# Four more units of y through DRAM, and the loads of turned k and q issued by ScalarE

## The chip, the cores and the metric

The kernel runs on one core of one Trainium2 chip. The metric is the device time of one execution in microseconds (us).

## The reference

Two blocks follow each other. The first is an mLSTM cell with gates, over 4 batches, 8 heads, 768 time steps and 40 values per head; the second is a feed-forward block on the 3072 tokens that come out, 320 values each.

```python
for t in range(S):
    m_new = np.maximum(f_gate[:, :, t] + m, i_gate[:, :, t])
    f_stab, i_stab = np.exp(f_gate[:, :, t] + m - m_new), np.exp(i_gate[:, :, t] - m_new)
    C = f_stab * C + i_stab * outer(v_t, k_t);  n = f_stab * n + i_stab * k_t
    h = C @ q_t;  denom = np.maximum(np.abs(n @ q_t), 1.0)
    y[:, :, t] = sigmoid(o_gate[:, :, t]) * h / denom
x = y as (3072, 320)
out = (((x @ w1) * (x @ w2)) @ w3) @ w_out        # w1, w2: 320 x 1024, w3: 1024 x 1024, w_out: 1024 x 320
```

All is float32.

## The kernel before

**Units and stages.** The tokens are cut into 24 units (n = 0 to 23) of 128 tokens: unit n is chunk n // 4 of batch n % 4. Four units make a group (gr = n // 4) of 512 tokens. One loop runs over stages s = 0 to 31. On TensorE, stage s does in this order: `x_trans` of an earlier unit (tile px, three 128x128 transposes), `fold` (tile wp: w3 times w_out, eight blocks of it in all), `up` and `up_rest` for groups 0 to 2 (tiles pa and pb), then `quarter_work(s)`: the output of unit s − 1 (tile cell, from pw, v and the state) and the scores and state products of unit s. So y of unit n leaves VectorE (line 445) in stage n + 1. TensorE's order is written down (`in_order`): each of its instructions follows the one before in the program. The other engines also run their instructions in the order in which they stand.

**The up products.** In stages 6 to 15 there are two `up` calls each. A call reads the turned x (tile xT) of two units at once: stages 12 and 13 read units 8 and 9, stages 14 and 15 units 10 and 11. Groups 3 to 5 are multiplied from stage 19 on by `up_by_seven` (a seven-product scheme), which needs sums of xT that `token_sums` makes on VectorE (line 666) when the group's last unit is turned. `up_by_seven` and `ffn_out` share the PSUM banks of the tile cell: ScalarE copies two products out of cell[1] (lines 704 and 702), after which `ffn_out` writes there.

**Two ways to turn y.** Units 0 to 14 go by `x_trans`: GpSimd repeats the last 64 columns (`twice`, line 476), TensorE transposes into PSUM (px, line 95), ScalarE copies to xT (line 486). In stages 10 and later `x_trans(n)` stands at the start of stage n + 3. Units 15 to 23 (`NY = 15`) go through DRAM: in stage n + 2, `send` writes y to y_d with four DMAs (lines 456 and 458), `get_back` reads it as 32-row blocks with four DMAs (tile yb, line 465), and `x_turn` transposes the blocks on VectorE (line 472). `x_turn` stands right before `turn(s + 1)`.

**Turned k and q.** From unit 10 on, `load_turned(n)` brings k and q in with eight DMAs (line 148), into one of two buffers (gates for even n, q_all for odd n), and `turn(n)` transposes them on VectorE (line 317). `load_turned(s + 2)` stands at the end of stage s, behind ScalarE's work of that stage: the a_sb copies (line 638), eight exponentials (pw, line 303), the gate (o_in, line 270) and, in stages up to 13, the scaling of raw weights (lines 191 and 195).

**Queues.** SP issues all loads and y_d transfers; ScalarE issues the stores of the output (line 743, `ffn_out`, from stage 16). In the built program the DMAs of both queues share eight completion counters, dealt out in turn. Each DMA carries a wait for the DMA that held its counter before.

Of the kernel before, what the change touches and what calls it, by code (L numbers as in the profile page):

```python
# [8 lines left out]
FP = mybir.dt.float32  # L9
# [7 lines left out]
def kernel(  # L17
# [26 lines left out]
    nc = tc.nc  # L44
# [3 lines left out]
    P = 128  # L48
    NT = S // L
    NT2 = S // P  # L50
    NU = NT2 * B
    NP = H // 2
# [16 lines left out]
    dram = ctx.enter_context(tc.tile_pool(name="dram", bufs=1, space=bass.MemoryType.DRAM))  # L69
# [7 lines left out]
    def mps(shape, name):  # L77
        pool = banks.pop(0)
        banks.append(pool)
        return pool.tile(shape, FP, name=name, tag="m")  # L80
# [13 lines left out]
    def transpose(out, in_, n=P):  # L94
        in_order(nc.tensor.transpose(out, in_, ident[0:n, 0:n]))  # L95
# [15 lines left out]
    N_DVE = N_U = 10  # L111
# [11 lines left out]
    decay = const.tile([P, B * NP, NT], FP, name="decay")  # L123
    UT = const.tile([P, 2, 3, BH], FP, name="UT")
    U_d = dram.tile([NT, BH, L], FP, name="U_d")
    NY = 15
    KC = KF + 1
    y_d = [dram.tile([P, 4, KC, 32], FP, name=f"y_d{n}") if n >= NY else None for n in range(NU)]

    o_t, u_t = {}, {}  # L130

# [9 lines left out]
    def load_turned(n):  # L141
        c, b = divmod(n, B)
        for dst, src in zip(turned_in[n % 2], (k, q)):
            for hip in range(2):
                of = src[b].rearrange("(p two) s d -> two p s d", two=2)[hip, :, c * P:(c + 1) * P, :]
                for j in range(2):
                    p0, c0 = hip * DP + j * 32, (1 - j) * 32
                    nc.sync.dma_start(out=dst[p0:p0 + 32, c0:c0 + NP * RAW].rearrange("r (p e) -> r p e", p=NP),  # L148
                                      in_=of.rearrange("p (r f) d -> r p (f d)", f=4))

    def load_o(n):
# [141 lines left out]
    def rows_of_u(n):  # L293
        c, b = divmod(n, B)
        nc.vector.transpose(out=weights_tile(n).rearrange("p h (t i) -> p h t i", t=2),
                            in_=UT[:, :, (0, 2, 1)[c], b * H:(b + 1) * H].rearrange("p t h -> p h t").unsqueeze(3).to_broadcast([P, H, 2, 32]))
# [14 lines left out]
    def turn(n):  # L311


        if n >= N_DVE:
            for src, dst, name in zip(turned_in[n % 2], (kT_t, qT_t), ("kT", "qT")):
                dst[n] = sb.tile([128, NP, P], FP, name=name, tag=name)
                done = nc.vector.transpose(out=dst[n].rearrange("i p (r f) -> i p f r", f=4),
                                           in_=src[:, 32:TB].rearrange("i (p f d) -> i p f d", p=NP, f=4)[:, :, :, 0:32])
            return done
        for src, dst, name in ((kbuf[n % NB], kT_t, "kT"), (qbuf[n % NBQ], qT_t, "qT")):  # L320
            pt = mps([128, NP, P], "pt")
            for p in range(NP):
                transpose(pt[:, p, :], src[:, 2 * p:2 * p + 2, :].rearrange("p a b -> p (a b)"))
            dst[n] = sb.tile([128, NP, P], FP, name=name, tag=name)
            nc.scalar.copy(out=dst[n], in_=pt)
# [7 lines left out]
    def decayed(new, old, n, x):  # L333
        c, b = divmod(n, B)
        nc.gpsimd.tensor_tensor(out=new, in0=old, op=OP.mult, in1=decay[:, b * NP:(b + 1) * NP, 2 * c + x:2 * c + x + 1]  # L335
                                .to_broadcast([P, NP, D1]))
# [114 lines left out]
    def send(n):  # L451


        y = y_t.pop(n)
        for cc in range(KF):
            nc.sync.dma_start(out=y_d[n][:, :, cc, :], in_=y[:, cc * P:(cc + 1) * P].rearrange("t (i c) -> t i c", c=32))
        for i in range(0, 4, 2):
            nc.sync.dma_start(out=y_d[n][:, i:i + 2, KF, :], in_=y[:, KF * P:DM].rearrange("t (i c) -> t i c", c=32))
# [3 lines left out]
    def get_back(n):  # L462
        back_t[n] = sb.tile([P, 4, KC, 32], FP, name="yb", tag="yb", bufs=1)
        for i in range(4):
            nc.sync.dma_start(out=back_t[n][32 * i:32 * (i + 1)].rearrange("r m k c -> r m (k c)"),
                              in_=y_d[n][:, i].rearrange("(m r) k c -> r m (k c)", r=32))

    def x_turn(n):
        gr, j = divmod(n, GT)
        if j == 0:  # L470
            x_t[gr] = ffn.tile([128, KC, TG], FP, name="xT", tag="xT")
        nc.vector.transpose(out=x_t[gr][:, :, j * P:(j + 1) * P].rearrange("c k (m r) -> c k m r", r=32),
                            in_=back_t.pop(n).rearrange("r m k c -> r k m c"))

    def twice(n):
        nc.gpsimd.tensor_copy(out=y_t[n][:, DM:DM + REM], in_=y_t[n][:, KF * P:DM])

    def x_trans(n):
        gr, j = divmod(n, GT)
        if j == 0:  # L480
            x_t[gr] = ffn.tile([128, KF + 1, TG], FP, name="xT", tag="xT")
        y = y_t.pop(n)
        px = mps([128, KF + 1, P], "px")
        for cc in range(KF + 1):
            transpose(px[:, cc, :], y[:, cc * P:(cc + 1) * P])
        nc.scalar.copy(out=x_t[gr][:, :, j * P:(j + 1) * P], in_=px)
# [5 lines left out]
    RAW = 4 * D  # L492
# [168 lines left out]
    def token_sums(gr):  # L661
        mem = wst.tile([128, FO, 128], FP, name="w3T", tag="w3T").rearrange("p k c -> p (k c)")
        T1, T2, T3, T4 = T_t[gr] = [mem[:, i * TH:(i + 1) * TH] for i in range(4)]
        (B11, B12), (B21, B22) = ([x_t[gr][:, cc, i * TH:(i + 1) * TH] for i in range(2)] for cc in range(KF))
        for dst, p, q in ((T1, B12, B11), (T2, B22, T1), (T3, B22, B12), (T4, B21, T2)):
            nc.vector.tensor_tensor(out=dst, in0=p, in1=q, op=OP.subtract)  # L666
# [96 lines left out]
    def ab_sums(gr, j):  # L763
        mem = [t.rearrange("p h d -> p (h d)") if j == 0 else io.tile([P, H, L], FP, name="pw", tag="pw", bufs=5)
               .rearrange("p h t -> p (h t)") for t in kbuf]
        S1, S2, S3, S4 = S_o[gr, j] = [t.rearrange("p (f t) -> p f t", t=P) for t in mem]
        (A11, A12), (A21, A22) = quarters_of_ab(gr, j)
        for dst, p, q, op in ((S1, A21, A22, OP.add), (S2, S1, A11, OP.subtract), (S3, A11, A21, OP.subtract),
                              (S4, A12, S2, OP.subtract)):
            nc.vector.tensor_tensor(out=dst, in0=p, in1=q, op=op)  # L770
# [47 lines left out]
    turned, converted, fetched = 0, 2, 5  # L818

    for s in range(len(n_up)):  # L820
        if NY <= s - 2 < NU:
            send(s - 2)
        if N_U <= s + 3 < NU:
            load_u(s + 3)
# [17 lines left out]
        if s < NU:  # L842
            if s >= B:
                decayed(state[s % B][1], state[s % B][0], s, 0)
        if s == 2 or N_DVE < s < NY + 2:
            twice(s - 2)
        if NY <= s - 2 < NU:
            get_back(s - 2)
        while s >= N_DVE and turned < min(s - 2, NY):
            x_trans(turned)  # L850
            turned += 1
        fold()
        if s >= len(n_up) - 2:
# [64 lines left out]
        with tc.issue_after(gated.ins) if gated else nullcontext():  # L918
            if seven:
                seven[3]()  # L920
            for _ in range({NU: 1, NU + 1: 3}.get(s, 0)):
                next(wsums)
            if s == NU + 1:
                ab_sums(*summed.pop(0))
            if NY <= s - 2 < NU:
                x_turn(s - 2)
            for n in () if s == 1 else (s + 2,) if s < B else (s + 2, s + 3) if s == B else (s + 3,):
                if n < N_U:
                    rows_of_u(n)
            if N_DVE <= s + 1 < NU:  # L930
                gated = turn(s + 1)
            if s - 2 in range(4 * GT - 1, NU, GT):
                token_sums((s - 2) // GT)
            if s < len(n_up) - 2 and n_out[s + 1] and s > NU + 2:
                ab_sums(*summed.pop(0))
# [8 lines left out]
        if s in (2, 3):  # L944
            turned, converted = 2, converted + (4 if s == 2 else 2)
        if s + 1 < N_DVE:
            while turned < min(s - 1, NY):
                x_trans(turned)
                turned += 1
            if s not in (1, 2):  # L950
                turn(s + 1)
# [22 lines left out]
        if N_DVE <= s + 2 < NU:  # L974
            load_turned(s + 2)
# [36 lines left out]
```

## Time and profile before

| | us |
|---|---|
| median of 3 runs | 425.77 |
| lowest and highest | 424.96, 426.05 |
| span of the profiled execution | 425.8 |
| TensorE busy | 414.1 |
| VectorE busy | 313.5 |
| GpSimd busy | 154.3 |
| ScalarE busy | 150.1 |
| mean share of the 16 DMA engines, SP's queue | 53.9% |

The profiled execution's span (first to last instruction) stands beside the median of the runs: they are the same to the digits shown. In the profile PE is TensorE's matmuls, PEld its weight loads, DVE VectorE, ACT ScalarE, POOL GpSimd, SP the engine that mostly issues DMAs; SPq and ACTq are DMA issues on these engines, and L with a number is a line of the kernel. Between 157 and 203 us a stage takes 15.3 us, in which TensorE is busy throughout.

### The profile page before, as it was taken

The page shows a single profiled execution, that of the slowest core. Times are in us where ns is not written, and L with a number is a line of the kernel's source. Part 1 is how long each engine was busy: PE and PEld are TensorE (multiplying, and loading weights), DVE is VectorE, ACT ScalarE, POOL GpSimd, SP SyncE. Part 2 cuts the span into 40 slices and gives each one's busy share as a digit, 9 for nine tenths or more (in the row PEclk, how much of TensorE's full clock was granted, in tenths as well). Part 3 has the DMA queues.
Part 4 walks back from the last instruction along what each step waited for, and adds up shares of the span by engine and source line. Part 5 has one row for each costly group of instructions (what it writes and reads, how often), then busy time and mean ns, then how long its engine had stood idle before and what let it go on. Part 6 is the DMA issues. An engine that isn't in the chain of part 4 may idle for free.

```text
span 425.8 us, 13079 instructions
## 1 busy us (share of the span) xinstructions
PE 414.1 (97%) x5353; PEld 335.3 (79%) x5353; DVE 313.5 (74%) x635; ACT 150.1 (35%) x404; POOL 154.3 (36%) x211
## 2 busy tenths in 40 slices
PE   7989989999999999999999999999999999999996
PEld 4768878888688788787777778788778879888896
DVE  6676986888949779778736966596868699575971
ACT  4766865567723623630433313032311110210000
POOL 4421342233303303303307751546453587542100
PEclk9989999999999999999999999999999999999999
DMA  8999998598977776985425675756421120000001
GB/s 186 204 173 245 214 144 140 134 193 180 215 183 154 166 182 135 181 164 105 89 80 130 153 141 121 142 133 117 87 44 36 35 39 2 31 2 31 2 32 62
DMA packets 135211, 51.15 MB, mean 120 GB/s; under 512 B 109360, under 2 KB 126960, under 8 KB 135152
## 3 DMA queue, kind: packets, MB, share of 16 engines
q1 hardware_dynamic: 131552, 46.29, 53.9%
q10 hardware_dynamic: 3600, 4.03, 2.7%
q8 instruction: 42, 0.69, 0.7%
q14 instruction: 17, 0.14, 0.1%
HBM read 44.50 MB, written 5.80 MB: 118 GB/s over the span
## 4 chain that ended last, share of the span: by engine, by line
PE 53%; issue 20%; DVE 7%; POOL 7%; SPq 7%; DMA 5%; ACT 1%; POOLq 0%; DVEq 0%
PE cell L92 17%; PE pa L92 12%; PE o L92 8%; PE pb L92 8%; PE p L92 3%; POOL pw L308 3%; SPq L184 3%; DVE w3T L666 2%; PE pt L95 1%; POOL vw L330 1%; SPq L148 1%; DMA raw<-in_moe_w_dram 1%; PE fill L92 1%; POOL raw L659 1%; POOL state L335 1%
## 5 line engine op out<-in xcount | busy, mean ns | idle before, releaser
L335 POOL TENSOR_TENSOR state<-state,decay 128x164 f32<-128x164 f32 x40 | 20.0, 500 | 154.8 <-DVE state L404 129.0
L92 PE MATMUL pa<-xT,w 128*128 128x256 f32 x240 | 60.4, 382 | 0.0
L92 PEld LDWEIGHTS pa<-xT,w 128*128 128x128 f32 x240 | 44.4, 190 | 6.8 <-DVE h L430 0.4
L303 ACT ACTIVATE pw<-pw,aT 128x64 f32<-128x64 f32 x184 | 46.4, 339 | 3.2 <-ACT o_sb L741 1.9
L92 PE MATMUL pb<-xT,w 128*128 128x256 f32 x192 | 45.4, 379 | 0.0
L729 POOL TENSOR_TENSOR ab<-ab,a_sb 128x512 f32<-128x512 f32 x22 | 29.4, 1356 | 32.2 <-DVE ab L684 32.2
L92 PEld LDWEIGHTS pb<-xT,w 128*128 128x128 f32 x192 | 36.4, 190 | 5.0
L711 POOL TENSOR_TENSOR wo<-wo 128x512 f32<-128x512 f32 x22 | 27.4, 1268 | 29.8 <-DVE wo L686 29.8
L92 PE MATMUL pa<-xT,wr 64*64 64x256 f32 x384 | 37.0, 386 | 0.5 <-DVE wr L200 0.5
L92 PE MATMUL wp<-wo,w3T 128*128 128x320 f32 x128 | 35.9, 433 | 1.1 <-DVE ab L639 0.6
L308 POOL TENSOR_SCALAR_AFFINE_SELECT pw<-pw 64x512 f32<-64x512 f32 x48 | 35.8, 746 | 3.0 <-ACT pw L303 1.2
L92 PE MATMUL pb<-xT,wr 64*64 64x256 f32 x384 | 36.4, 380 | 0.0
L92 PE MATMUL cell<-w3o,ab 128*128 128x320 f32 x128 | 35.4, 432 | 0.0
L638 ACT ACTIVATE a_sb<-pa 128x512 f32<-128x512 f32 x24 | 14.3, 598 | 59.0 <-PE pb L92 59.0
L639 DVE TENSOR_TENSOR ab<-pb,a_sb 128x512 f32<-128x512 f32 x24 | 16.4, 688 | 23.2 <-ACT a_sb L638 22.8
L92 PEld LDWEIGHTS wp<-wo,w3T 128*128 128x128 f32 x128 | 23.8, 190 | 10.5 <-DVE ab L639 0.8
L92 PEld LDWEIGHTS cell<-w3o,ab 128*128 128x128 f32 x128 | 24.3, 190 | 9.5
L92 PEld LDWEIGHTS pa<-xT,wr 64*64 64x64 f32 x384 | 18.9, 132 | 15.4 <-issue 8.8
L686 DVE SCALAR_TENSOR_TENSOR a_sb<-pa,wo 128x512 f32<-128x512 f32 x12 | 8.3, 689 | 29.8 <-PE pa L92 29.8
L430 DVE TENSOR_TENSOR h<-cell,h 64x164 f32<-64x164 f32 x88 | 28.6, 326 | 1.6
L92 PE MATMUL po<-w3o,ab 128*128 128x320 f32 x96 | 26.4, 433 | 0.0
L92 PEld LDWEIGHTS po<-w3o,ab 128*128 128x128 f32 x96 | 18.1, 190 | 7.3
(180 smaller groups left out, 846.4 us busy)
## 6 DMA issues: line engine op xcount, KB each, us to landing
raw<-in_moe_w_dram SPq DMA_DIRECT2D x64, 128.0 KB, 3.4
kbuf<-in_k_dram SPq DMA_DIRECT2D x24, 160.0 KB, 4.5
v_all<-in_v_dram SPq DMA_DIRECT2D x24, 160.0 KB, 4.9
o_in<-in_o_gate_dram SPq DMA_DIRECT2D x24, 160.0 KB, 4.8
pw<-U_d SPq DMA_DIRECT2D x28, 128.0 KB, 3.5
raw<-in_moe_w_dram SPq DMA_DIRECT2D x5, 512.0 KB, 6.7
raw<-in_moe_w_out_dram SPq DMA_DIRECT2D x8, 320.0 KB, 4.1
gates<-in_k_dram SPq DMA_DIRECT2D x28, 80.0 KB, 2.5
```

Source lines behind the costliest of these rows:

```text
L92: in_order(nc.tensor.matmul(out, lhsT=lhsT, rhs=rhs, start=start, stop=stop))
L184: nc.sync.dma_start(out=dst, in_=src)
L303: nc.scalar.activation(out=pw[:, h, :], in_=src[:, h, :], func=AF.Exp, bias=aT[:, c, b * H + h:b * H + h + 1])
L308: nc.gpsimd.affine_select(out=pw[r], in_=pw[r], compare_op=OP.is_ge, fill=0.0, base=0, pattern=[[0, H], [1, L]], channel_multiplier=-1)
L335: nc.gpsimd.tensor_tensor(out=new, in0=old, op=OP.mult, in1=decay[:, b * NP:(b + 1) * NP, 2 * c + x:2 * c + x + 1] .to_broadcast([P, NP, D1]))
L430: nc.vector.tensor_tensor(out=part, in0=ph[x][halves[e]], in1=part, op=OP.add)
L638: nc.scalar.mul(out=a_sb, in_=pa, mul=UP ** -2)
L639: nc.vector.tensor_tensor(out=ab_t[gr][j][:, fs[0]:fs[-1] + 1, t0:t0 + a_sb.shape[-1]], in0=pb, in1=a_sb, op=OP.mult)
L666: nc.vector.tensor_tensor(out=dst, in0=p, in1=q, op=OP.subtract)
L686: nc.vector.scalar_tensor_tensor(out=out, in0=p, scalar=UP ** -2, in1=q, op0=OP.mult, op1=OP.add)
L711: aside_by.tensor_tensor(out=kept[j][:, 1:4:2], in0=kept[j][:, 1:3], in1=kept[j][:, 3:4].to_broadcast([128, 2, TH]), op=OP.add)
L729: aside_by.tensor_tensor(out=t[:, f:FO:FH, :], in0=t[:, f:FO:FH, :], in1=a, op=OP.mult)
```

## The change

Unit 10 and units 12 to 14 join units 15 to 23 on the way through DRAM (`Y_BACK`), so of the units from 10 on only unit 11 still goes by `x_trans`. `x_turn` moves from before `turn(s + 1)` to behind it, for all units that go this way. The eight DMAs of `load_turned(n)` are issued by ScalarE instead of SP for n from 13 on.

```diff
-    NY = 15
+    Y_BACK = [10] + list(range(12, NU))
     KC = KF + 1
-    y_d = [dram.tile([P, 4, KC, 32], FP, name=f"y_d{n}") if n >= NY else None for n in range(NU)]
+    y_d = [dram.tile([P, 4, KC, 32], FP, name=f"y_d{n}") if n in Y_BACK else None for n in range(NU)]
...
-                    nc.sync.dma_start(out=dst[p0:p0 + 32, c0:c0 + NP * RAW].rearrange("r (p e) -> r p e", p=NP),
+                    (nc.sync if n < 13 else nc.scalar).dma_start(out=dst[p0:p0 + 32, c0:c0 + NP * RAW].rearrange("r (p e) -> r p e", p=NP),
                                       in_=of.rearrange("p (r f) d -> r p (f d)", f=4))
...
-        if NY <= s - 2 < NU:
+        if s - 2 in Y_BACK:
             send(s - 2)
...
-        if s == 2 or N_DVE < s < NY + 2:
+        if s == 2 or N_DVE < s < NU + 2 and s - 2 not in Y_BACK:
             twice(s - 2)
-        if NY <= s - 2 < NU:
+        if s - 2 in Y_BACK:
             get_back(s - 2)
-        while s >= N_DVE and turned < min(s - 2, NY):
-            x_trans(turned)
+        while s >= N_DVE and turned < min(s - 2, NU):
+            if turned not in Y_BACK:
+                x_trans(turned)
             turned += 1
...
-            if NY <= s - 2 < NU:
-                x_turn(s - 2)
             for n in () if s == 1 else (s + 2,) if s < B else (s + 2, s + 3) if s == B else (s + 3,):
                 if n < N_U:
                     rows_of_u(n)
             if N_DVE <= s + 1 < NU:
                 gated = turn(s + 1)
+            if s - 2 in Y_BACK:
+                x_turn(s - 2)
...
-            while turned < min(s - 1, NY):
+            while turned < s - 1:
                 x_trans(turned)
                 turned += 1
```

## The prediction

> **What bounds the kernel now.** I read the page first: who is busy, and where.
>
> ```profile
> span 425.8 us, 13079 instructions
> ...
> PE 414.1 (97%) x5353; PEld 335.3 (79%) x5353; DVE 313.5 (74%) x635; ACT 150.1 (35%) x404; POOL 154.3 (36%) x211
> ```
>
> TensorE is busy for 414.1 of 425.8 us, so a gain is work taken off it and a loss is a wait put before it. ScalarE's 35% is a mean; what matters is when its results are due. So next come the timelines of TensorE and ScalarE where stage 13 ends and stage 14 begins. Columns: start us, us, line, what, xcount, and in brackets the idle time before.
>
> ```profile
> 174.22 0.55 PE L95 MATMUL px<-ident,y 128*128 128x128 f32 x3
> 174.61 4.47 PE L92 MATMUL wp<-wo,w3T 128*128 128x320 f32 x16
> 178.92 1.89 PE L92 MATMUL pa<-xT,w 128*128 128x256 f32 x8
> ...
> ```
>
> ```profile
> 177.08 0.67 ACT L195 ACTIVATE raw<-raw 128x512 uint32<-128x512 uint32 x1
> 177.64 0.46 ACT L486 COPY xT<-px 128x384 f32<-128x384 f32 x1
> ```
>
> TensorE transposes y of unit 11 (px), does wp, and at 178.92 reads the xT that ScalarE has copied by 178.10. Margin: 0.82 us. Stage 12 has the same with unit 9: copy 146.35 to 146.82, pa at 148.34, margin 1.52 us. `up` reads the tokens of two units, so in the stages where a pair begins (12 and 14) nothing of it can start without this copy.
>
> Third, what a DMA costs the engine that issues it, in the view of waits of SP and ScalarE's timeline:
>
> ```profile
> SPq L465 <- DMA out_dram<-o_sb: 11.0, 4, 4.8
> ```
>
> ```profile
> 240.41 0.34 ACTq L743 DMA_DIRECT2D out_dram<-o_sb  x1
> 240.87 2.02 ACT L303 ACTIVATE pw<-pw,aT 128x64 f32<-128x64 f32 x8 [0.49 <-DMA y_d<-y]
> ```
>
> SP's reads of y_d waited 11.0 us for stores of the output, and ScalarE beside one of its own stores for a write of y_d; the data have nothing to do with each other. It is the eight completion counters: an issue stands until the earlier holder of its counter, on either queue, has landed. What stands behind it on that engine stands too.
>
> **The change part by part.**
>
> *TensorE loses 12 transposes.* The steps from px to the next matmul are 0.38 us for unit 10 (158.94 to 159.32) and 0.39 us each for units 12, 13 and 14 (189.51, 204.80, 220.07). TensorE has no idle time there, so all of it counts: −1.55 us, in stages 13, 15, 16 and 17.
>
> *ScalarE loses four xT copies* (0.47 us) and GpSimd four copies of 0.24 us. Neither set the end there: 0.
>
> *VectorE gains four transposes* of 0.57 us (5.1 us / 9 in the group L472). They lie in stages 12, 14, 15, 16, before VectorE's idle times of 2.15, 2.13, 7.59 and 3.53 us: 0. Without that cover they would cost 2.3 us together.
>
> *x_turn behind k and q* for units 15 to 23. One instruction changes places with two; before L666 their sum is the same, so TensorE's wait for L666 (0.41 us at 242.83) stays. The 1.40 us that VectorE waited for yb at 249.54 are hidden by 2 us of k and q, but VectorE then waits 4.87 us for TensorE anyway: 0.
>
> *SP* loses 88 issues (11 units x 8) of 0.45 us and gains 32. It has room: it waits 18.7 us for y alone. The four new sends do enter a queue that ran ahead: send(12) waits for y(12), and what stands behind it (loads for two stages later, get_back) follows late but in time.
>
> *ScalarE gains the 88 issues.* This is the part with a price. In the order of the built program the eight of unit 13 stand between the last `raw` and the xT copy of unit 9, those of unit 15 between `raw` and the copy of unit 11. One costs 0.45 us (four took 1.80 us on SP in quiet stages) and lands 2.4 us after issue, if its counter is free.
>
> Stage 12. The first five follow each other from 146.40; the last three use counters of the first three of the same eight and wait for those to land. The third is issued at 147.30, lands at 149.7 (2.4) or 150.8 (3.5, the k loads' median at 140 to 190 us); then the eighth issues, 0.45, and the copy, 0.47. Copy done at 150.6 to 151.7 against 148.34: 2.3 to 3.4 us. I take 2.6, nearer to the first, since half of the eight are q loads, which landed in 2.3.
>
> Stage 14, in times of before (y(12), ScalarE and TensorE all move with the shift). The last two of the eight use counters held before by the third and fourth DMA of send(12). These start only when y(12) leaves VectorE at 179.30 (L445, 178.48 + 0.82): two issues of 0.64, one of 0.57, the fourth at 181.15, issue over at 181.7. It lands 1.8 us after its start or its end: 183.0 to 183.5. Then 0.45 for the eighth issue, 0.46 for the copy, 0.1 for passing on: 184.0 to 184.5 against 178.92, so 5.1 to 5.6 us; I take 5.2. If no counter were waited for, 8 x 0.45 − 0.82 = 2.8 us.
>
> Stages 13, 15 and 16: only the wp copy stands behind the eight. Its bank is wanted 5 us later: 0.
>
> Stage 19: ScalarE's copy of the first product (L704) runs from 247.02 to 247.62, and TensorE writes that bank at 248.55, a margin of 0.93. Behind the eight of unit 20 (4.65 us, the last on a counter of the batch's fifth: 1.8 + 2.4 + 0.45) after o_in at 243.26, L704 ends at 248.5, just in time. But o_in will be later: pw stands behind an output store whose counter load_u(21) held, and that is issued behind send(16), whose y comes at 235.83. Sends to 238.6, landing 3.5, store 0.4, pw and o_in 2.4: 244.9; + 4.65 + 0.6 = 250.2 to 250.5, so 1.9 us of wait; between 0 (store not held) and 3.5 (a second store held as well). Stages 20 to 22 have this margin without two stores in a row: 0, at most 2 together.
>
> *The clock after a wait.* The windows show TensorE's busy time, granted clock, DMA share and GB/s:
>
> ```profile
> 21.00:24.00 3.00, 1.81 (x32) 0.90 1.14 129
> 24.00:27.00 3.00, 3.00 (x34) 0.53 1.03 160
> 27.00:30.00 3.00, 3.00 (x65) 1.00 0.99 153
> 57.00:60.00 3.00, 1.51 (x62) 1.00 0.60 82
> 60.00:63.00 3.00, 3.00 (x19) 1.00 1.23 220
> ```
>
> After 1.19 us of idle at 21.8 the clock was halved for some 3.4 us, which costs half of it, 1.7 us; after 1.49 us at 57.6 it was not. So short waits sometimes pay this. I put one such period behind the longest wait: 1.7 us; bounds 0 and 3.4.
>
> The Trainium skill, "TensorE: Matmul & The Clock Gate", section "What's actually happening", lets the clock fall only after a whole idle window of about 3.4 us; the row at 24.00 speaks against it. By that rule the waits of stages 12 and 19 cost nothing more, and that of stage 14 the same 1.7.
>
> Sum: 425.8 − 1.55 + 2.6 + 5.2 + 1.9 + 1.7 = 435.6 us. The span is the median (425.77), so no correction.
>
> A rule speaks against the move as such. The skill's "DMA: Bandwidth & Descriptors", section "Issuing engines are not separate DMA queues", says that issuing from more engines saves only the sequencer's time, usually small beside the transfer. Read as "issuing costs nothing worth counting", it would leave the sum at 424.2; by the rows above it does not hold here, because the issues stand in front of a copy that TensorE waits for.
>
> **The rivals.**
>
> *Faster, 424.2 us.* The copies still come in time, and only the −1.55 remains. Decided by the eight issues: they must take under 0.82 us in stage 14, 0.10 each, and under 1.52 us in stage 12. For it: ScalarE is only 35% busy, and it was always ahead of pa. Against it: ScalarE's own stores took 0.34 us each before any wait.
>
> *Issues, but no waits for counters: 428.3 us.* Eight issues take 2.7 us at the 0.34 of ScalarE's stores or 3.6 at SP's 0.45. Stage 12 loses 1.2 to 2.1 us, stage 14 1.9 to 2.8, less 1.55, clock and stage 19 at 0: 427.3 to 429.2. For it: most counters will be free. Against it: the SP row above, and send(12) cannot be early.
>
> *Waits everywhere: 442 us.* Stage 12 at 3.4, stage 14 at 5.7, stage 19 at 3.5, 2 in stages 20 to 22, two halved clocks of 1.7: 425.8 − 1.55 + 14.6 + 3.4 = 442.
>
> That the change does not do what it says is excluded by the built order, which shows the twelve transposes gone and the 88 issues on ScalarE.
>
> **How the numbers follow.** Forecast (waits for counters and for send(12), 432 to 438.5): 0.70. Waits everywhere (over 438.5): 0.12. No waits for counters (427.1 to 432): 0.11. Faster: 0.05. Within 0.3%: 0.02. 0.3% is 1.28 us, about what a measurement of this kernel can tell from no change (the three runs span 1.09 us). The predicted time is the forecast's, 435.6. The range leaves out the faster case and a little at each end: 429 to 441. Slower by over 0.3%: 0.70 + 0.12 + 0.11 = 0.93.
>
> **What would show it.** Right: TensorE idle before the first pa of stages 12 and 14, released by ScalarE's L486, 2 to 3 and 5 to 6 us; eight L148 issues on ScalarE ahead of that copy; the copies of stages 13 and 15 without effect; some idle before the cell<-w3o,ab of stage 19; four px groups gone. The forecast is wrong if TensorE's idle time stays near 11 us (the faster rival), if the stage 14 wait is under 3 us (the counter did not hold ScalarE), or if the loss lies on VectorE, waiting for yb.

## The result and the profile after

| | before | after |
|---|---|---|
| median, us | 425.91 (4 runs beside those of after) | 442.09 (4 runs, 440.60 to 445.37) |
| ratio of the times, 95% interval | | 1.040 (1.036 to 1.044) |
| profiled execution: span, us | 425.8 | 443.6 |

The change makes the kernel slower by 16 us. The forecast was 435.6 us and its range ended at 441: the direction was right, and so was the kind of loss (DMA issues on ScalarE in front of copies that TensorE waits for); the size was not. The profiled execution of after took 445.37 us, 1.8 us more than its span; the steps below compare span with span, 425.8 with 443.6.

The page of after, span and busy time of each engine:

```profile
span 443.6 us, 13121 instructions
...
PE 419.5 (95%) x5341; PEld 337.7 (76%) x5341; DVE 315.3 (71%) x639; ACT 149.0 (34%) x400; POOL 154.6 (35%) x207
```

TensorE runs 12 instructions fewer and is busy for 5.4 us longer (414.1 before). That can't be work, so part of it must run at a lower clock. Its idle time grew by 12.4 us (443.6 − 419.5 against 425.8 − 414.1). The view of waits says behind what; its columns are us in total, times, longest:

```profile
PE pa L92 <- ACT xT L486: 7.3, 2, 5.8
PE cell L92 <- ACT wo L702: 4.6, 1, 4.6
PE pa L92 <- DVE w3T L666: 0.4, 1, 0.4
```

The first two lines are new, the third was there before. To see in which stages the time is lost, take the start of `quarter_work(s)` on TensorE (the group cell<-v_all,pw) in both timelines, and its distance to the next one:

| from quarter_work of | before, us | after, us | difference |
|---|---|---|---|
| stage 11 (start) | at 141.13 | at 142.84 | +1.71 |
| 11 to 12 | 15.99 | 17.87 | +1.88 |
| 12 to 13 | 15.28 | 15.01 | −0.27 |
| 13 to 14 | 15.29 | 24.01 | +8.72 |
| 14 to 17 | 41.47 | 40.62 | −0.85 |
| 17 to 18 | 10.69 | 10.68 | −0.01 |
| 18 to 19 | 19.18 | 25.78 | +6.60 |
| 19 to 20 | 18.45 | 18.45 | 0 |

The first row lies ahead of everything that the change touches, so it is the spread of one execution against another. The other rows say where the change acts: three stages lose 17.2 us, and the units that no longer pass TensorE give back 1.12 us.

Stage 14 in TensorE's timeline, the answer to the rows that the prediction opened with:

```profile
177.53 0.55 PE L95 MATMUL px<-ident,y 128*128 128x128 f32 x3
177.92 4.47 PE L92 MATMUL wp<-wo,w3T 128*128 128x320 f32 x16
188.17 3.78 PE L92 MATMUL pa<-xT,w 128*128 128x256 f32 x8 [5.78 <-ACT xT L486]
191.74 2.83 PE L92 MATMUL pb<-xT,w 128*128 128x256 f32 x8
```

pa follows wp after 5.78 us, not at once, and then takes 3.78 us where it took 1.89. ScalarE's timeline for the same time shows what it did instead of the copy (ACTq rows are DMA issues, counted apart from its own instructions):

```profile
179.83 0.66 ACT L191 ACTIVATE raw<-raw 128x512 f32<-128x512 f32 x1
180.39 0.66 ACT L195 ACTIVATE raw<-raw 128x512 uint32<-128x512 uint32 x1
180.89 3.65 ACTq L148 DMA_DIRECT2D q_all<-in_k_dram  x2
184.58 3.02 ACTq L148 DMA_DIRECT2D q_all<-in_q_dram  x4
187.64 0.48 ACT L486 COPY xT<-px 128x384 f32<-128x384 f32 x1 [6.59 <-DMA q_all<-in_q_dram]
```

The px that the copy reads was ready at 178. The copy stands behind eight issues, six of which are seen here; in quiet places one took 0.32 to 0.45 us, so four take 1.8 at most and two 0.9. The rest, at least 2.7 and 1.2 us, is ScalarE standing at an issue.

What it stood for can be read too: the trace's records have the completion counter of each DMA, and when each DMA landed.

| issue of unit 15 | starts at | DMA that held its counter before, and its issue | landed at |
|---|---|---|---|
| third k | 180.89 | load of pw, SP, 176.80 | 180.87 |
| fourth k | 184.22 | load of v_all, SP, 178.57 | 184.20 |
| third q | 186.79 | third DMA of send(12), SP, 183.92 | 186.77 |
| fourth q | 187.19 | fourth DMA of send(12), SP, 184.59 | 187.17 |

Each of the four starts 0.02 us after the earlier holder has landed, and then takes 0.32 to 0.41 us itself. So ScalarE waits for counters here, and the last two are those of send(12) that the prediction named.

The windows of TensorE over the same stage (us, PE busy with its instructions, granted clock, DMA share, GB/s) show the second loss, the clock, at 0.50 where before had 1.00:

```profile
184.00:188.00 4.00, 0.00 (x0) 0.85 0.79 142
188.00:192.00 4.00, 3.83 (x9) 0.50 1.13 189
192.00:196.00 4.00, 4.00 (x16) 0.80 0.38 59
```

Stage 19 on ScalarE, first before, then after:

```profile
247.02 0.60 ACT L704 ACTIVATE wo<-cell 128x512 f32<-128x512 f32 x1 [3.77 <-PE cell L92]
247.51 0.58 ACT L702 COPY wo<-cell 128x512 f32<-128x512 f32 x1
```

```profile
255.25 0.46 ACT L270 ACTIVATE o_in<-o_in 128x320 f32<-128x320 f32 x1
257.98 2.26 ACTq L148 DMA_DIRECT2D gates<-in_k_dram  x3
260.44 2.86 ACTq L148 DMA_DIRECT2D gates<-in_q_dram  x4
263.40 0.60 ACT L704 ACTIVATE wo<-cell 128x512 f32<-128x512 f32 x1 [7.70 <-DMA gates<-in_q_dram]
263.90 0.58 ACT L702 COPY wo<-cell 128x512 f32<-128x512 f32 x1
```

TensorE writes that bank (the products of `ffn_out`) after the second of the two copies:

```profile
264.53 5.73 PE L92 MATMUL cell<-w3o,ab 128*128 128x320 f32 x14 [4.63 <-ACT wo L702]
```

From the end of o_in to the first copy 7.7 us pass; the issues themselves are some 3 of them.

### The profile page after: what moved, and what is told of

It is laid out like the page before. It is cut to its first block, busy times and chain, and to the rows that moved or that the text cites. A ratio compares the mean times of both kernels' runs of the same rounds, so it can differ in the third digit from the quotient of the medians.

```text
span 443.6 us, 13121 instructions
## 1 busy us (share of the span) xinstructions
PE 419.5 (95%) x5341; PEld 337.7 (76%) x5341; DVE 315.3 (71%) x639; ACT 149.0 (34%) x400; POOL 154.6 (35%) x207
## 3 DMA queue, kind: packets, MB, share of 16 engines
HBM read 45.29 MB, written 6.59 MB: 117 GB/s over the span
## 4 chain that ended last, share of the span: by engine, by line
PE 64%; issue 11%; DVE 8%; DMA 6%; SPq 6%; POOL 2%; ACT 1%; ACTq 0%; DVEq 0%; POOLq 0%
PE cell L92 18%; PE pa L92 15%; PE pb L92 10%; PE o L92 8%; PE p L92 4%; PE po L92 4%; DMA v_all<-in_v_dram 2%; PE wp L92 2%; SPq L184 2%; DVE w3T L666 1%; PE pt L95 1%; DMA yb<-y_d 1%; DVE pw L770 1%; POOL pw L308 1%; PE fill L92 1%
## 5 line engine op out<-in xcount | busy, mean ns | idle before, releaser
L92 PE MATMUL pa<-xT,w 128*128 128x256 f32 x240 | 63.9, 400 | 7.3 <-ACT xT L486 7.3
L92 PEld LDWEIGHTS pa<-xT,w 128*128 128x128 f32 x240 | 46.5, 199 | 15.3 <-ACT xT L486 8.3
L92 PE MATMUL pb<-xT,w 128*128 128x256 f32 x192 | 46.3, 385 | 0.0
L92 PE MATMUL cell<-w3o,ab 128*128 128x320 f32 x128 | 37.2, 448 | 4.6 <-ACT wo L702 4.6
L92 PEld LDWEIGHTS pb<-xT,w 128*128 128x128 f32 x192 | 37.4, 195 | 5.5
L729 POOL TENSOR_TENSOR ab<-ab,a_sb 128x512 f32<-128x512 f32 x22 | 29.4, 1359 | 32.0 <-DVE ab L684 32.0
```

The source lines that it names most:

```text
L92: in_order(nc.tensor.matmul(out, lhsT=lhsT, rhs=rhs, start=start, stop=stop))
L729: aside_by.tensor_tensor(out=t[:, f:FO:FH, :], in0=t[:, f:FO:FH, :], in1=a, op=OP.mult)
```

## The experiments

The theory after this: all of the loss comes from the 88 issues on ScalarE, and of these from 24, those of units 13, 15 and 20, which stand in front of copies that TensorE waits for. The rivals: the four added trips of y through DRAM load SP and VectorE; the order of x_turn; the number of issues rather than their place. "After" and "before" in the edits name the kernel that was edited.

**1. The trips of y without the issues.** After, with SP issuing everything:

```diff
-(nc.sync if n < 13 else nc.scalar).dma_start(
+nc.sync.dma_start(
```

> The changed kernel, but SP issues all DMAs of turned k and q (the DRAM route of units 10 and 12 to 14, and x_turn behind k and q, stay). Theory (the loss is ScalarE's sequencer held by completion counters in front of copies that TensorE waits for): no waits in stages 12, 14 and 19, what remains is the twelve transposes, measured in the trace after at 0.28 us per stage, 1.1 us in all: 425.9 - 1.1 = 424.8. Rival (the loss comes from the DRAM route itself: more small packets, later yb, a later VectorE): still slower than before by several us, 430 or more, with VectorE waiting for yb.

Measured: 430.04 us, ratio 1.011 (1.008 to 1.014). A miss for the theory; the trips are not free on SP, as the rival had it. TensorE's waits and VectorE's:

```profile
PE pa L92 <- DVE w3T L666: 4.2, 1, 4.2
```

```profile
DVE xT L472 <- DMA yb<-y_d: 13.3, 5, 6.6
```

VectorE waited 1.4 us for yb before and 0.7 us after; here it is 13.3. SP issues the read back of unit 15 only at 235.47, 13 us after y(15) was ready (221.31 + 0.82): SP is full. VectorE turns it late, the sums of L666 come late, and TensorE waits 4.2 us, with a lower clock behind it. So ScalarE's issues do relieve something. TensorE does not wait for L486 in this kernel: stage 14 takes 15.30 us and stage 12 16.44 (before: 15.29 and 15.99).

**2. The issues without the trips.** Before, with the same line as after:

```diff
-nc.sync.dma_start(
+(nc.sync if n < 13 else nc.scalar).dma_start(
```

> The kernel before, with only one edit: ScalarE issues the DMAs of turned k and q from unit 13. Theory: the waits of stages 12 and 19 stay (1.7 us, and 4.8 with 1.8 of halved clock), that of stage 14 is shorter because no send(12) is in the counters (about 3 instead of 5.9, perhaps without the clock): 425.9 + 9 to 13 = 435 to 439. Rival (the DRAM route costs): 426, within 1 us of before.

Measured: 440.51 us, 1.036 (1.033 to 1.040), slower than expected. TensorE's waits:

```profile
PE pa L92 <- ACT xT L486: 5.7, 2, 4.3
PE cell L92 <- ACT wo L702: 4.6, 1, 4.6
```

The same two waits as in after. The issues alone make 15 of the 16 us (stage 14 takes 6.3 us more than before, stage 19 8.0), and they do so where the added sends of y (send(12) among them) don't exist.

**3. Order of x_turn alone.** Before, with `x_turn` behind `turn`:

```diff
-            if NY <= s - 2 < NU:
-                x_turn(s - 2)
             for n in () if s == 1 else (s + 2,) if s < B else (s + 2, s + 3) if s == B else (s + 3,):
...
                 gated = turn(s + 1)
+            if NY <= s - 2 < NU:
+                x_turn(s - 2)
```

> The kernel before, with only one edit: x_turn stands behind turn(s + 1) instead of before it, for units 15 to 23. Theory: VectorE's 1.4 us wait for yb is hidden by k and q but TensorE sets the end of these stages: 425.1 +- 0.5. Rival (x_turn later makes token_sums later): up to 1 us slower.

Measured: 425.62 us, 0.999 (0.997 to 1.002). Nothing, as forecast.

**4. Unit 15 off ScalarE.** After, with one unit given back to SP:

```diff
-(nc.sync if n < 13 else nc.scalar).dma_start(
+(nc.sync if n < 13 or n == 15 else nc.scalar).dma_start(
```

> The changed kernel, but SP issues the eight DMAs of unit 15. Theory: the wait of stage 14 (5.9 us, and 2.8 us of halved clock behind it) goes, the others stay: 442.1 - 8.7 = 433.4. Rival (each batch of eight issues on ScalarE costs about the same, some 1.5 to 2 us for each of eleven): 440 to 441.

Measured: 434.09 us, 1.022 (1.018 to 1.025): 8.0 us back, stage 14's share of the table to within 0.7; stage 14 takes 15.29 us again, while stage 19 takes 1.2 us more than in after. In the waits only one of L486 is left, stage 12's:

```profile
PE cell L92 <- ACT wo L702: 5.0, 1, 5.0
PE pa L92 <- ACT xT L486: 1.0, 1, 1.0
```

**5. Unit 20 off ScalarE.** The same edit with `n == 20`.

> The changed kernel with unit 20's k and q alone issued by SP again. In the changed kernel stage 19 cost 6.6 us: a wait of 4.63 us for the second copy into wo (L702), and 1.8 to 2.0 us of halved clock behind it. Theory (the eight of unit 20, held in ScalarE's queue, delay both copies): that wait is gone, the waits of stages 12 and 14 stay (1.5 and 5.8 us), and the time is 442.1 - 6.6 = 435.5 us. Rival (the copies are late because o_in and pw come late, behind SP's sends and an output store, whoever issues unit 20): a wait of at least 2 us stays at the start of stage 20's first product, and the time is 438.5 us or more.

Measured: 433.97 us, 1.020 (1.017 to 1.022): 8.1 us back, 1.5 more than expected. From quarter_work of stage 18 to that of 19 this kernel takes 19.17 us, as before (19.18), and the waits show stages 12 and 14 as they were, with L702 nearly gone:

```profile
PE pa L92 <- ACT xT L486: 7.8, 2, 5.9
PE cell L92 <- ACT wo L702: 0.4, 1, 0.4
```

So stage 19 is those eight issues, and not a late o_in: o_in ends 5.6 us behind the start of stage 18's quarter_work here, in after 4.7. The 1.5 us beyond are not in that stage; the profiled span lies 10.8 us below that of after, of which 4.5 us are there already at stage 11, so most of it is probably spread between executions.

**6. Units 13, 15 and 20 off ScalarE, the other 64 issues left there.** The same edit with `n < 14 or n in (15, 20)`.

> The changed kernel, but SP issues the DMAs of units 13, 15 and 20; ScalarE still issues the 64 of the other eight units. Theory (the place in ScalarE's order decides: only these three batches stand in front of a copy that TensorE waits for): the waits of stages 12, 14 and 19 go with the halved clock behind them, 442.1 - 1.7 - 8.7 - 6.6 = 425.1, if SP, with 24 issues more, still brings yb in time; up to 429 if it does not. Rival (the number of issues on ScalarE decides): 8/11 of the loss stay, 437.5.

Measured: 426.31 us, 1.002 (1.001 to 1.004). Place decides, not number: 64 of 88 issues on ScalarE cost at most 1.2 us beside the expected 425.1. And that 1.2 us has another source. In ScalarE's timeline of stage 14 there is no issue at all:

```profile
176.08 0.69 ACT L191 ACTIVATE raw<-raw 128x512 f32<-128x512 f32 x1 [2.14 <-DMA raw<-in_moe_w_dram]
176.67 0.65 ACT L195 ACTIVATE raw<-raw 128x512 uint32<-128x512 uint32 x1
177.22 0.45 ACT L486 COPY xT<-px 128x384 f32<-128x384 f32 x1
```

The copy now stands behind a late load of raw weights: VectorE had waited 3.1 us for y of unit 10 (166.65), so the weight buffers came free late, and SP loaded them late. Stage 14 takes 16.89 us, 1.6 more than before; experiment 12 tests this reading.

**7. Is stage 14's hold that of send(12)?** The prediction let the last of unit 15's issues wait for counters of that send, and so for y(12). After, with unit 12 left to TensorE:

```diff
-Y_BACK = [10] + list(range(12, NU))
+Y_BACK = [10] + list(range(13, NU))
```

> The changed kernel, but unit 12 goes by TensorE again, so there is no send(12) whose DMAs hold the counters of unit 15's batch. Theory: the wait of stage 14 falls from 5.9 us to about 3 (issue and older loads alone) and the clock is perhaps not halved: 442.1 - 3 to 5.7 = 436.4 to 439, the transposes of one unit added (0.3). Rival (plain issue time of the eight): the wait stays at 5.9, 442.4.

Measured: 442.22 us, 1.041 (1.037 to 1.045). A miss: no send(12), and yet the wait is no shorter (6.49 us in stage 14, against 5.78).

```profile
PE pa L92 <- ACT xT L486: 8.1, 2, 6.5
PE cell L92 <- ACT wo L702: 5.3, 1, 5.3
```

Eight issues follow each other over eight counters that are dealt out in turn, among SP's loads, so taking one holder away puts another in its place. By the counters in this kernel's trace, the fourth issue starts at 181.37, 0.02 us after a load of kbuf has landed, and the eighth at 185.75, 0.02 us after a load of pw; the copy follows at 186.11. So the prediction had the holder of after right, but the wait did not hang on it.

**8. Half of the issues.** After, with only the four k loads of unit 15 on ScalarE:

```diff
-(nc.sync if n < 13 else nc.scalar).dma_start(
+(nc.sync if n < 13 or n == 15 and src is q else nc.scalar).dma_start(
```

> The changed kernel with only the four k loads of unit 15 on ScalarE, its four q loads on SP. It tells the time that issuing takes from the time that an issue stands for a completion counter. By the deal of the counters, the third and fourth k load follow a load of pw and one of kbuf, which are issued about 3 and 2 us before and land 4 to 5 us after their issue. Theory (counters): the copy into xT still waits for the fourth issue, TensorE waits 1.0 to 2.2 us at the start of stage 14, and the time is 442.1 - 8.7 + (1.5 to 3) = 435 to 436.5 us. Rival (issue time alone, 0.42 us each): 4 x 0.42 = 1.7 us behind raw, of which 0.8 us were margin and the sequencer runs ahead of raw: a wait of 0 to 0.3 us, and 433.4 to 434.1 us, as without unit 15.

Measured: 435.46 us, 1.022 (1.020 to 1.024). The wait is 0.59 us, between the two expectations. ScalarE's timeline:

```profile
175.88 1.68 ACTq L148 DMA_DIRECT2D q_all<-in_k_dram  x2
177.61 0.48 ACT L486 COPY xT<-px 128x384 f32<-128x384 f32 x1 [1.40 <-PE wp L92]
```

Two issues take 1.68 us, against 0.97 for the two before them: some 0.7 us of hold. The same two, third and fourth k of unit 15, took 3.65 us in after. By the counters in the traces the third follows a load of pw in both kernels. The fourth follows a load of v_all in after, issued at 178.57 and landed at 184.20, and one of kbuf here, issued at 172.82 and landed at 177.23; both start 0.02 us later. So the 3.65 us are a hold by the holder, and not issuing time; but the size that I expected of it here was too large. The total fell into the expected 435 to 436.5 for another reason: stage 19's wait was 6.4 us in this execution.

**9. The same issues, behind the copies.** After, with the eight of each unit one stage later, ahead of `ffn_out` and behind the copies L486, L704 and L702:

```diff
+        if 13 <= s + 1 < NU:
+            load_turned(s + 1)
         if seven and s <= NU:
             ffn_out(
...
-        if N_DVE <= s + 2 < NU:
+        if N_DVE <= s + 2 < 13:
             load_turned(s + 2)
```

> The changed kernel, but ScalarE's eight issues for a unit stand one stage later and behind that stage's copies (xT and w3o, or the two product copies), in the stretch in which ScalarE waits for TensorE. All 88 issues stay on ScalarE. Theory (place): no waits in stages 12, 14 and 19, SP is still relieved so that yb is in time; what remains is the transposes saved, 1.1 us: 425.9 - 1.1 = 424.8. Rival (number of issues, or the DRAM route): 430 or more.

Measured: 435.97 us, 1.024 (1.020 to 1.029). A miss. The old waits are gone but for 1.0 us (L486), and two new ones are there:

```profile
PE cell L92 <- POOL ab L729: 3.1, 1, 3.1
PE cell L92 <- ACT o_sb L741: 3.0, 1, 3.0
```

```profile
249.63 4.74 ACTq L148 DMA_DIRECT2D gates<-in_k_dram  x4
256.31 4.15 ACTq L148 DMA_DIRECT2D gates<-in_q_dram  x4
260.51 0.43 ACT L741 COPY o_sb<-cell 128x320 f32<-128x320 f32 x1 [12.82 <-DMA yb<-y_d]
```

The eight of unit 20 now keep the copy o_sb waiting, which empties the bank that TensorE wants for the next `quarter_work` (it goes on at 261.86). In stage 21 the wait is put down to GpSimd's L729, but it ends the same way: the eight of unit 22 are out at 300.30, o_sb is copied from 300.40 to 300.83, and TensorE goes on at 300.92. These stages and the clock behind the waits cost 11.6 us in the profiled execution, stage 14 another 2.2. In this part of the kernel there is always a copy behind the issues.

**10 and 11. What is the clock in stage 14's 8.72 us?** After, with fill products for TensorE between wp and pa of stage 14, so that it isn't idle while it waits. First 13 of them, then, since each took 0.87 us instead of the expected 0.43 and they outlasted the wait, 6:

```diff
         fold()
+        if s == 14:
+            warm(13)          # second run: warm(6)
```

> The changed kernel, with 13 matmuls of 128x512 on the identity (0.43 us each) put before the up products of stage 14; their result is not used. They fill the wait there. Theory (the clock is halved because TensorE idles): the wait stays as long but the clock is not halved behind it: 442.1 - 2.8 = 439.3. Rival (the slow matmuls after the wait come from something else, the transfers of that time): no change or slower, 442 to 443.

> The changed kernel with 6 fill products (6 x 0.87 = 5.2 us) between wp and pa of stage 14, where TensorE waits 5.78 us; 13 of them lasted 11.3 us, 5.6 us more than that wait, and gave 444.07 us with the clock at 1.00 throughout. Theory (2.8 us of stage 14's 8.7 us are the clock that halves after the idle time, and the fill replaces idle time only): a rest of 0.3 to 0.8 us of wait stays, the clock stays at 1.00 between 184 and 200 us, pa's first eight take 1.89 us instead of 3.78 us, and the time is 442.1 - 2.8 = 439.3 us. Rival (the 2.8 us are not the clock's, or the fill moves something else): 441.5 to 442.6 us.

Measured: 444.07 us, 1.043 (1.038 to 1.048), and 442.09 us, 1.039 (1.034 to 1.043). The 13 fills lasted 11.32 us and held pa back by 5.6 us beyond the copy; less these, 444.07 would be 438.5, but that is only argued. The 6 fit. TensorE's wait and the windows of that kernel:

```profile
187.09 1.99 PE L92 MATMUL pa<-xT,w 128*128 128x256 f32 x8 [0.61 <-ACT xT L486]
```

```profile
184.00:188.00 4.00, 3.39 (x10) 1.00 0.84 155
188.00:192.00 4.00, 4.00 (x21) 1.00 1.15 183
192.00:196.00 4.00, 4.00 (x47) 1.00 0.10 23
```

The clock stays at 1.00, and stage 14 takes 21.32 us against 24.01, 2.7 us less, as the theory had it. The total did not move, as the rival had it: in the profiled execution stages 12 and 15 took 0.35 us more each and stage 19 took 0.96 us more (its wait 5.3 us). Its four runs lie between 439.58 and 445.21 us, so a gain of 2.7 us in the total could neither be seen nor ruled out well. The clock's part of stage 14 is shown; that it can be had as time is not.

**12. A version meant to beat both.** Units 12 to 14 through DRAM, unit 10 by TensorE as before (its trip made experiment 6 late), and ScalarE issuing only units 14, 16 to 19 and 21 to 23. After, with:

```diff
-Y_BACK = [10] + list(range(12, NU))
+Y_BACK = list(range(12, NU))
...
-(nc.sync if n < 13 else nc.scalar).dma_start(
+(nc.sync if n < 14 or n in (15, 20) else nc.scalar).dma_start(
```

> A version meant to beat both: y of units 12 to 14 through DRAM and VectorE, y of unit 10 by TensorE as before; SP issues k and q up to unit 13, and of 15 and 20; ScalarE issues the other units. The version with y of unit 10 through DRAM too lost 1.6 us in stage 14, where weights arrived 2.1 us late because VectorE had waited 3.1 us for y of unit 10. Theory: without that trip no wait is left, and the time is that of before less three units' transposes, 3 x 0.28 = 0.84 us: 424.8 us (0.2% faster). Rival (SP is too full in stages 11 to 13 with units 13 and 15 on it, whichever y is read back): a wait of 0.5 to 1 us stays in stage 14, and the time is 425.6 to 426.5 us.

Measured: 424.48 us (11 runs) against 425.52 of before (16 runs), 0.997 (0.996 to 0.999). Faster by 0.3% (expected: 0.2%). TensorE waits for neither L486 nor L702; from quarter_work of stage 11 to that of stage 24 it takes 192.13 us against 192.88, 0.75 less. The kernel differs from that of experiment 6 in unit 10's way alone, and stage 14 takes 15.29 us again: it was that trip which made the weights late.

## Why the prediction was right and wrong

From 435.6 to the span of 443.6 are 8.0 us. By the steps of the sum:

| step | forecast | measured | short by |
|---|---|---|---|
| early part, not touched | 0 | 1.7 | 1.7 |
| transposes saved | −1.55 | −1.1 | 0.4 |
| stage 12 | 2.6 | 1.9 | −0.7 |
| stage 14 with clock | 5.2 + 1.7 | 8.7 | 1.8 |
| stage 19 | 1.9 | 6.6 | 4.7 |

**The step that failed is stage 19.** The eight issues of unit 20 in front of the copies were named, but their term was sized at 1.9 us and measured 6.6; experiment 5 shows that all 6.6 hang on these eight. Three things were missing behind o_in. The eight kept the copy back for 7.7 us, not 4.65: the prediction followed their counters only within the batch (the last on that of the fifth, which is so), while the second to the fifth waited for DMAs ahead of it. They start at 257.98, 259.31, 259.92 and 260.44, 0.02 to 0.08 us after an output store, a load of o_in and two reads of yb have landed. TensorE waits for the second copy, L702, not for L704, 0.5 us earlier: the prediction's margin of 0.93 us was read from the wrong copy. And a wait of 4.63 us pays the clock as well, about 2 us (6.60 − 4.63), which the sum put behind the longest wait only. The upper bound of 3.5 left out the first two.

Up to o_in the time was right and its reason only half. The prediction had o_in end at 244.9 in before's time; with the 11.2 us by which after lags behind at the start of stage 18 this is 256.1, and it ended at 255.7. The forecast cause was a store that waits for the counter of load_u(21). That load landed at 252.72, but the copy in front of the store ended only at 252.88, since the eight of unit 19 had kept ScalarE:

```profile
251.53 0.43 ACT L741 COPY o_sb<-po 128x320 f32<-128x320 f32 x1 [6.64 <-DMA q_all<-in_q_dram]
...
252.45 0.43 ACT L741 COPY o_sb<-po 128x320 f32<-128x320 f32 x1 [0.49 <-PE cell L92]
252.91 0.37 ACTq L743 DMA_DIRECT2D out_dram<-o_sb  x1
```

The store did not wait. Unit 19's eight were not in the sum; that the two paths meet within 0.2 us is luck.

**Stage 14 was right in its wait, and short by the clock.** 5.78 us against 5.2, and the last two issues were held by send(12) as forecast (186.77 and 187.17 in the table of the result). What the prediction did not see is that other DMAs hold as long: v_all kept the fourth issue until 184.20 in after, and without send(12) the wait stays (experiment 7). The clock cost 2.7 us (experiment 11), not 1.7. The prediction took its price from a period in which TensorE had been granted half the clock for 3.4 us; here it was halved or partly so from 188 to 194 us.

**Stage 12 was too dear.** The wait is 1.53 us, since ScalarE issued ahead of its own instructions (that this made the difference is argued, not tested):

```profile
143.56 1.05 ACT L303 ACTIVATE pw<-pw,aT 128x64 f32<-128x64 f32 x4
144.36 0.34 ACTq L148 DMA_DIRECT2D q_all<-in_k_dram  x1
...
146.94 0.67 ACT L191 ACTIVATE raw<-raw 128x512 f32<-128x512 f32 x1
...
149.07 2.18 ACTq L148 DMA_DIRECT2D q_all<-in_q_dram  x4
151.29 0.48 ACT L486 COPY xT<-px 128x384 f32<-128x384 f32 x1 [3.12 <-DMA q_all<-in_q_dram]
```

In the program the issues stand behind the second raw pair, in the chip the first went out at 144.36, during the exponentials. The prediction started all of them at 146.40. What held here was again a DMA ahead of the batch: the fifth issue starts at 149.07, 0.02 us after a load of v_all has landed.

The Trainium skill, "Perfetto Trace Analysis", section "Per-engine timelines", describes both halves of this: an instruction of ScalarE is pushed into a queue and the sequencer reads on, while an instruction that the sequencer carries out itself keeps it until its semaphores are satisfied. This case's rows agree: four issues overtook raw instructions, and a held issue kept back a copy that had its data (187.64, 6.59 us).

**"SP has room" was wrong** for the trips of y alone: experiment 1 costs 5 us (430.04 against 425.07 of before on the same chip). It did no harm here, since the change also takes 88 issues away from SP. **Transposes** gave 0.27 to 0.29 us a unit, not 0.38: their price was taken from the distance from px to the next group, and the table shows that some 0.1 us of it stays when px goes. **x_turn, VectorE, stages 13, 15 and 16** at 0 were right (experiment 3; the table). **The span as the median** was loose: the executions of after have times 1.7 to 1.8 us above their spans, so before's profiled one was probably one of its slower ones; that explains none of the 8 us, but the forecast of a median owed it a word.

**The rival "waits everywhere", 442 us,** has the measured median almost to the digit, but not by its terms. It gave stage 12 3.4 us, stage 19 3.5, and stages 20 to 22 2 more; the table has 1.9 and 6.6, and from stage 19 to 20 both kernels take 18.45 us. Its number is luck.

The rule on issuing engines that the prediction weighed (issues save or cost only the sequencer's time) leads to 424.2; experiment 2 puts the move at 15 us. Experiment 6 shows where the rule does hold: 64 issues with no copy behind them that TensorE waits for cost little.

**What stays open.** Stage 12's eight were not undone alone. Why stage 19's wait ranges from 3.9 us (experiment 10) to 6.4 (experiment 8) between these kernels wasn't followed, nor why some holders take so long to land: the load of o_in issued at 252.25 landed at 259.29.

## What to carry to other kernels

Before DMA issues move to a compute engine, list what stands behind each batch on that engine and who waits for it; idle time in the mean says nothing, 24 of 88 issues made nearly all of the loss. Price a batch by its holders: where DMAs share completion counters, an issue waits for the earlier user of its counter, a neighbour on another queue with other data, and in experiment 7 removing one holder only promoted the next. Moving the batch behind the copy that suffered helps only if no other copy follows; taking single batches away from the engine did.

## What the runs showed of the hardware

The description of the kernel has the engines run their instructions in the order in which they stand. For a DMA issue that held only against what comes later, not against unfinished instructions of the engine ahead of it: ScalarE's first k load went out at 144.36, 2.6 us before the second raw pair, which stands in front of it, started (146.94).

The clock: idle times of 1.53 us (after, stage 12), 1.84 and 2.04 us (experiments 5 and 11, stage 12) left it at 1.00. Idle times of 4.18, 4.63 and 5.78 us were followed by 0.5. So were 3.04 us in experiment 9, TensorE's windows there:

```profile
260.00:264.00 4.00, 2.14 (x80) 0.74 0.42 135
264.00:268.00 4.00, 4.00 (x66) 0.50 0.03 6
```

The Trainium skill, "TensorE: Matmul & The Clock Gate", section "What's actually happening", wants a whole idle window of about 3.4 us for that. The 3.04 us are below it, and so were before's 1.19 us, though there two shorter idle times (0.34 and 0.41 us) lay close ahead. As a rough rule of these runs, 2 us were safe from stage 12 on and 3 us were not.
